# A reordered start in a fused attention and feed-forward kernel: scaling of q, its scores, a padded copy of v and one addition change places

## The chip, the cores and the metric

The kernel runs on one core of one Trainium2 chip, alone. The metric is the device time of one execution in microseconds (us). Four runs of the kernel before gave a median of 559.15 us (557.59 to 560.10).

Five engines work side by side on a core, each with its own queue of instructions: TensorE (PE, with its weight loads shown as PEld), VectorE (DVE), ScalarE (ACT), GpSimd (POOL) and SyncE (SP), which here only issues transfers. Transfers (DMAs) are issued from SP's queue and from ACT's queue.

## The reference

A gated linear attention over 4 batches, 8 heads, 768 tokens and a head size of 48, followed by a two-layer network with an ELU between the layers:

```python
f = 1.0 / (1.0 + np.exp(-f_logit))
for t in range(S):
    state = f[:, :, t, :, None] * state + np.einsum('bhd,bhe->bhde', k[:, :, t], v[:, :, t])
    y[:, :, t] = np.einsum('bhd,bhde->bhe', q[:, :, t], state)
x = y.transpose(0, 2, 1, 3).reshape(B * S, H * D)
h = x @ w_in                                   # 384 -> 2048
g = np.where(h > 0.0, h, np.exp(np.minimum(h, 0.0)) - 1.0)
out = g @ w_out                                # 2048 -> 384
```

The two weight matrices arrive in 64-bit floats; the rest in 32-bit floats.

## The kernel before, in words

The 3072 tokens are cut into 12 units of 256, three to a batch. A unit goes through attention and then through the network; the attention of the next unit is woven between the steps of the network of the one before. Only the start is a stretch without a network to weave into: there the attention of unit 0 has to be finished first. The order of the instructions at the start is written out by hand in `fast` (lines 1079 to 1154); the change lies in it. Later steps are placed by `at_step`.

How attention is computed. Instead of the recurrence, running products of the gates are used. With a = 1 + exp(-f_logit), the running product of a over the tokens of a unit is 1 over the running product of the gates. k is multiplied by it, q by its inverse; then scores are plain products of k and q under a causal mask, and states are plain sums of k times v. The heads lie in four pairs (0 to 3). The tile `f` holds, for each pair, the running product (index 0) and its inverse (index 1). Pair 3 has no rows of its own in the loaded f_logit: its gates arrive packed in the gap rows of pairs 0 to 2 and are spread into place by small transfers.

The helpers that the change and the prediction speak of:

- `gates(u, pieces, bias)` (L612): ACT computes exp(-f) in place (L617) and, unless `bias` is 0, adds one in a second ACT instruction (L619).
- `grow(u, p)` (L628): DVE's running product of pair p (L631). `fall(u, p)` (L633): DVE's inverse of it (L636, 128x256, about 1.7 us each).
- `move(u, which, queue)` (L638): two small transfers (L643) that spread pair 3's running product (`which` 0) or inverse (`which` 1), issued on the queue named.
- `scale(u, ("k" or "q", p, engine))` (L622): k or q of pair p times `f`, in place (L626), here always on POOL.
- `transposed(u, h, bank, pairs)` (L667): PE transposes k (L674), ACT copies the result to `kn` (L678).
- `advance(u, pairs)` (L727): PE's products of `kn` and v, the growth of the states (L737). `step(u, c)` (L686): the states of the four chunks of 64 tokens, one after the other (ACT L697 for the first, DVE L695).
- `scores(u, banks, pairs, pc)` (L703): PE's products of k and q (L714). `mask(u, pc)` (L720): DVE multiplies them by the causal mask (L722); the last part of the scores has to be there.
- `warm(n)` (L1068): n dummy products on PE (L1074) whose result nobody reads; each is two instructions in the profile.
- `first_outputs(part)` (L788): the outputs of unit 0, from masked scores and v in part 0, from states in part 1 (L817). Pair 3's share uses `padded_v` and `padded_s`, copies of v and of the states between columns of zeros, made by POOL (L1113 and L1136); `even_v` (L1098) is another copy of v. ACT and DVE then copy the outputs into `xt` (L827, L829).
- `load(u, names)` (L435): SP's loads of a unit's f, k, q and v. `fetch(n)` (L539): SP's transfer of a piece of the weights into `area`, a staging tile of 7 places (L549, L551, L554). `split`, `lower` and `merge` (L561 to L587) turn such a piece from 64-bit into 32-bit floats, on DVE, ACT and DVE.

What sets the order around the change. Every engine takes its instructions in the order of the program. `fetch(0)` and `fetch(1)` are issued early. The next five stand behind a memset on POOL that clears a few words of `area` (L1142), which in turn stands on POOL behind the last `scale` of unit 0's q and the three copies to `padded_s`. Each transfer signals one of eight semaphores, which are handed out in turn; a transfer that gets a semaphore still in use waits until the transfer before it on that semaphore has landed. The feed-forward network begins with the first up projection (L949), which needs `xt` of unit 0 and the first merged piece of `w_in`. From the second unit on the up projection is split into seven products (L904) on differences of `xt` that POOL makes (`blend`, L892).

Of the kernel before, what the change touches and what calls it, by code (L numbers as in the profile page):

```python
# [356 lines left out]
def fast(ctx: ExitStack, tc: tile.TileContext, q, k, v, f_logit, w_in, w_out, out, flag, outer):  # L357
# [18 lines left out]
    nc = tc.nc  # L376
# [12 lines left out]
    NKT = DM // 128  # L389
# [36 lines left out]
    qkf = [  # L426
        {n: cst.tile([128, HP, 2, U] if n == "f" else [128, HP, U], FP32, name=f"{n}{i}") for n in "fqk"}
        for i in range(NB)
    ]
# [182 lines left out]
    def gates(u, pieces=(NKT,), bias=1):  # L612

        p = 0
        for n in pieces:
            a = qkf[u % NB]["f"][:, p : p + n, 0]
            nc.scalar.activation(a, a, AF.Exp, scale=-1.0)  # L617
            if bias:
                nc.scalar.activation(a, a, AF.Copy, bias=1.0)  # L619
            p += n  # L620

    def scale(u, *todo):  # L622

        t = qkf[u % NB]
        for n, p, e in todo:
            e.tensor_tensor(out=t[n][:, p], in0=t[n][:, p], in1=t["f"][:, p, "kq".index(n)], op=ALU.mult)  # L626

    def grow(u, p):  # L628

        g = qkf[u % NB]["f"][:, p, 0]  # L630
        nc.vector.tensor_tensor_scan(out=g, data0=g, data1=g, initial=1.0, op0=ALU.mult, op1=ALU.max)  # L631

    def fall(u, p):  # L633

        f = qkf[u % NB]["f"]
        nc.vector.reciprocal(f[:, p, 1], f[:, p, 0])  # L636

    def move(u, which, queue):  # L638

        f = qkf[u % NB]["f"]  # L640
        for r in range(2):
            to = PAD + D * r
            queue.dma_start(out=f[to : to + D, NKT, which], in_=f[GAP[r] : GAP[r] + PAD, 0:NKT, which])  # L643
# [23 lines left out]
    def transposed(u, h, bank, pairs=(0, 1)):  # L667

        pairs = [p for p in pairs if u < 2 or 2 * h + p < NKT]
        if 0 in pairs:  # L670
            pts[u, h] = ps.tile([128, 2, NW, 128], FP32, tag=bank, name=f"psT{u}_{h}")
        for p in pairs:
            for w in range(NW):
                nc.tensor.transpose(  # L674
                    pts[u, h][:, p, w], in_=qkf[u % NB]["k"][:, 2 * h + p, w * W : (w + 1) * W], identity=ident[:]
                )
        p, to = slice(pairs[0], pairs[-1] + 1), slice(2 * h + pairs[0], 2 * h + pairs[-1] + 1)
        nc.scalar.copy(kn[:, to], pts[u, h][:, p])  # L678
        if u < 2:
            return  # L680
        gaps = kn[:, NKT, :, MAIN].rearrange("t w (r i j) -> t j w r i", r=2, j=NKT)
        nc.scalar.copy(gaps[:, to], pts[u, h][:, p].rearrange("t p w (a i) -> t p w a i", i=PAD)[:, :, :, 0::7])
# [20 lines left out]
    def scores(u, banks=("a0", "a1"), pairs=range(HP), pc=None):  # L703

        t = qkf[u % NB]
        if pc is None:
            ats[u] = sb.tile([128, 2, NW, HP, C], FP32, tag="at", name=f"at{u}", bufs=1)
            pc = [ps.tile([128, NW, HP, C], FP32, tag=banks[r], name=f"psS{u}_{r}") for r in range(2)]
        for p in pairs:
            for w in range(NW):  # L710
                for b in range(2):
                    cols = slice(w * W + b * C, w * W + b * C + C)
                    for r in range(2):
                        nc.tensor.matmul(  # L714
                            pc[r][FULL[b], w, p], lhsT=t["k"][FULL[r], p, cols], rhs=t["q"][FULL[r], p, cols],
                            start=True, stop=True,
                        )
        return pc
# [8 lines left out]
    def advance(u, pairs=range(HP)):  # L727

        if u not in pus:
            pus[u] = [ps.tile([128, NW, HP, D], FP32, tag=n, name=f"psU{u}_{n}") for n in ("a0", "a1")]  # L730
        pu = pus[u]
        for p in pairs:
            for w in range(NW):
                for r in range(2):
                    h = 2 * p + r
                    for b in range(2):
                        nc.tensor.matmul(  # L737
                            pu[b][FULL[r], w, p], lhsT=kn[FULL[b], p, w, FULL[r]],
                            rhs=vs[u % NB][FULL[b], w, PAD + h * D : PAD + (h + 1) * D],
                            start=(w == 0 and p == 0), stop=(w == NW - 1 and p == HP - 1), skip_group_check=True,  # L740
                        )
# [326 lines left out]
    def warm(n, bank="m0", small=0):  # L1068

        pw = ps.tile([128, 4, 128], FP32, tag=bank, name="psW")  # L1070
        for _ in range(small):
            nc.tensor.matmul(pw[0:1, 0, 0:1], lhsT=ident[:, 0:1], rhs=ident[:, 0:1], start=True, stop=True)
        for _ in range(n):
            nc.tensor.matmul(  # L1074
                pw[:], lhsT=ident[:], rhs=ident[:].unsqueeze(1).broadcast_to([128, 4, 128]), start=True, stop=True
            )
# [15 lines left out]
    fall(0, 0)  # L1092
    scale(0, ("q", 0, nc.gpsimd))
    warm(WA, "m3")
    gates(1, bias=0)
    advance(0, (0, 1))
    pc = scores(0, ("m2", "m3"), (0,))
    nc.gpsimd.tensor_copy(  # L1098
        even_v[:, :, :, PAD:],
        vs[0][:, :, PAD : PAD + NKT * 2 * D].rearrange("t w (p r d) -> t w p r d", r=2, d=D)[:, :, :, 0],  # L1100
    )
    fall(0, 1)
    scale(0, ("k", NKT, nc.gpsimd), ("q", 1, nc.gpsimd))
    fall(0, 2)
    move(0, 1, nc.scalar)
    warm(4)
    transposed(0, 1, "m1", (1,))
    advance(0, (2,))
    scores(0, None, (1,), pc)
    scale(0, ("q", 2, nc.gpsimd))  # L1110
    advance(0, (3,))
    scores(0, None, (2,), pc)
    nc.gpsimd.tensor_copy(  # L1113
        padded_v[:, :, :, PAD : 2 * PAD].rearrange("t w (r j) k -> t w r j k", r=2),
        vs[0][:, :, PAD + NKT * 2 * D : PAD + DM].rearrange("t w (r k j) -> t w r j k", r=2, j=NKT),
    )
    a = qkf[1]["f"][:, 0:NKT, 0]
    nc.vector.tensor_scalar_add(a, a, 1.0)
    for p in range(NKT):
        grow(1, p)  # L1120
    move(1, 0, nc.sync)
    scale(0, ("q", NKT, nc.gpsimd))
    warm(2)
    scores(0, None, (NKT,), pc)
    warm(1)
    fall(1, 0)
    split(0)
    for c in range(NC - 1):
# [88 lines left out]
def kernel(tc, q, k, v, f_logit, w_in, w_out, out):  # L1217

    nc = tc.nc
    with tc.tile_pool(name="flags", bufs=1) as pool:
        flag = pool.tile([1, 1], I32, name="flag")
        store = fast(tc, q, k, v, f_logit, w_in, w_out, out, flag, pool)
        seen = nc.values_load(flag[0:1, 0:1])
        with tc.If(seen < 128) as branch:
            general(tc, q, k, v, f_logit, w_in, w_out, out)
        with branch.Else():
            store(nc.sync, nc.scalar)  # L1230
# [32 lines left out]
```

## Time and profile before

| what | value |
|---|---|
| median of 4 runs | 559.15 us |
| the profiled execution | 558.88 us |
| its span, first to last instruction | 557.1 us |
| PE busy | 541.5 us, 97% |
| DVE busy | 406.9 us, 73% |
| POOL busy | 290.4 us, 52% |
| ACT busy | 228.0 us, 41% |
| granted TensorE clock | 0.999 |
| HBM read, written | 45.02 MB, 4.72 MB |
| chain that ended last | PE 85%, DMA 8%, DVE 3% of the span |
| first up projection (L949) begins | 28.86 us |
| first split product that waits (L904) | 74.83 us |

How to read it. The span is that of one profiled execution, the time is that of the same execution as the host of the runs counts it; they differ by 1.8 us. A row of a timeline gives start, duration, engine, line, operation, output and input tiles and how many; in brackets stands the idle time before it and what ended that. A row of the waits gives who waited for whom: us in total, times, longest. A row of the chain gives start, duration and what held the end at that time. A row of the windows gives the stretch, its length, busy time and count of instructions of PE, PEld, DVE, ACT and POOL, the granted clock, the mean busy share of the 16 DMA engines (which can read slightly over 1) and GB/s. Where an instruction waits for several things, the profile names the one that came last by its own records, and that can be another than the program waits for.

### The profile page before, as it was taken

To read this page: it belongs to the slowest core of one execution; us is meant where nothing else is said; L and a number is where in the kernel's file an instruction comes from. 1 tells how busy PE (TensorE), PEld (TensorE's weight loads), DVE (VectorE), ACT (ScalarE), POOL (GpSimd) and SP (SyncE) were. 2 spreads that over 40 slices of the span, in tenths; PEclk is the share of its full clock that TensorE was granted. 3 is DMA by queue.
4 is the path that set the end of the run, shared out by engine and by line. 5 is a ranking of instruction groups with operands and counts; after the bars stand their busy time and mean duration, and the time that the engine had idled before them with its cause. 6 is when DMAs were issued, how large, how long until landed. Compare 5 with 4: busy or idle time off the path is not lost.

```text
span 557.1 us, 15617 instructions
## 1 busy us (share of the span) xinstructions
PE 541.5 (97%) x6358; PEld 506.6 (91%) x6358; DVE 406.9 (73%) x804; ACT 228.0 (41%) x443; POOL 290.4 (52%) x559
## 2 busy tenths in 40 slices
PE   6799999999999999999999999999999999999996
PEld 3477769999999999999999999999999999999995
DVE  8888997997676776776785785785786687745553
ACT  3288765333434344343434434343343334333331
POOL 6600787484573474375365466357267257325332
PEclk9999999999999999999999999999999999999999
DMA  8998971042034134226216207207308302301001
GB/s 212 253 254 220 290 184 45 4 93 79 3 89 136 35 83 141 63 46 169 73 27 181 81 11 195 81 8 192 88 8 191 88 9 72 88 5 33 31 2 35
DMA packets 39474, 54.30 MB, mean 97 GB/s; under 512 B 4032, under 2 KB 29216, under 8 KB 39392
## 3 DMA queue, kind: packets, MB, share of 16 engines
q1 hardware_dynamic: 38592, 52.61, 36.4%
q8 instruction: 52, 0.85, 0.6%
q10 hardware_dynamic: 800, 0.59, 0.4%
q14 instruction: 30, 0.25, 0.2%
HBM read 45.02 MB, written 4.72 MB: 89 GB/s over the span
## 4 chain that ended last, share of the span: by engine, by line
PE 85%; DMA 8%; DVE 3%; POOL 1%; issue 1%; SPq 1%; ACT 1%; DVEq 0%; ACTq 0%; POOLq 0%
PE psH L904 39%; PE psM L1015 37%; DMA area<-in_moe_w_in_dram 3%; DMA f<-f 2%; PE psY L752 2%; PE psY L772 2%; PE psU_a L737 2%; PE psS L714 2%; PE psT L674 1%; DMA xt<-xt 1%; PE psM L981 1%; DMA f<-in_f_logit_dram 1%; DMA area<-in_moe_w_out_dram 1%; DVE f L636 1%; DVE bits L568 0%
## 5 line engine op out<-in xcount | busy, mean ns | idle before, releaser
L904 PE MATMUL psH<-xt,wi 128*128 128x128 f32 (+1 forms) x1056 | 195.0, 294 | 0.0
L968 POOL TENSOR_TENSOR sums<-gg 128x128 f32<-128x128 f32 x172 | 75.7, 461 | 206.2 <-DVE gg L958 188.7
L936 ACT ACTIVATE gg<-hh 128x512 f32<-128x512 f32 x88 | 55.5, 631 | 248.9 <-DVE hh L926 108.7
L904 PEld LDWEIGHTS psH<-xt,wi 128*128 128x128 f32 x1056 | 149.5, 192 | 1.6
L904 PE MATMUL psH<-xt,area 128*128 128x128 f32 x704 | 121.6, 275 | 1.2 <-POOL xt L892 1.2
L904 PEld LDWEIGHTS psH<-xt,area 128*128 128x128 f32 x704 | 106.5, 191 | 6.0 <-POOL xt L892 1.4
L913 DVE TENSOR_TENSOR hh<-psH,u 128x256 f32<-128x256 f32 x88 | 36.9, 419 | 97.6 <-ACT u L911 97.5
L1015 PE MATMUL psM<-area,sums 128*128 128x192 f32 x516 | 99.9, 326 | 0.1
L1015 PEld LDWEIGHTS psM<-area,sums 128*128 128x128 f32 x516 | 86.0, 190 | 0.3 <-issue 0.2
L1015 PE MATMUL psM<-wo,gg 128*128 128x192 f32 x376 | 77.7, 332 | 0.0
L958 DVE SCALAR_TENSOR_TENSOR gg<-gg,hh 128x512 f32<-128x512 f32 x88 | 63.5, 722 | 1.5 <-ACT gg L937 1.5
L636 DVE RECIPROCAL f<-f 128x256 f32<-128x256 f32 x36 | 62.8, 1748 | 1.3
L937 ACT ACTIVATE gg<-gg 128x512 f32<-128x512 f32 x96 | 60.5, 631 | 3.0
L1015 PEld LDWEIGHTS psM<-wo,gg 128*128 128x128 f32 x376 | 60.2, 190 | 1.3
L926 DVE TENSOR_TENSOR hh<-psH,u43h 128x256 f32<-128x256 f32 (+1 forms) x176 | 54.7, 353 | 3.0
L626 POOL TENSOR_TENSOR q<-q,f 128x256 f32<-128x256 f32 x48 | 40.0, 835 | 20.5 <-DMA area<-in_moe_w_in_dram 14.8
L968 POOL TENSOR_TENSOR sums<-gg,sums 128x128 f32<-128x128 f32 x86 | 45.1, 525 | 6.7
L626 POOL TENSOR_TENSOR k<-k,f 128x256 f32<-128x256 f32 x48 | 40.5, 846 | 8.9 <-DMA f<-f 6.2
L926 DVE TENSOR_TENSOR u43h<-psH,hh 128x256 f32<-128x256 f32 x88 | 37.0, 421 | 9.2 <-PE psH L904 8.8
L968 POOL TENSOR_TENSOR sums<-sums,gg 128x128 f32<-128x128 f32 x86 | 42.6, 495 | 0.0
L1015 PE MATMUL psM<-area,gg 128*128 128x192 f32 x172 | 42.0, 326 | 0.0
L1015 PE MATMUL psM<-wo,sums 128*128 128x192 f32 x172 | 42.0, 326 | 0.0
(102 smaller groups left out, 645.1 us busy)
## 6 DMA issues: line engine op xcount, KB each, us to landing
area<-in_moe_w_out_dram SPq DMA_DIRECT2D x8, 768.0 KB, 10.5
again<-in_moe_w_in_dram SPq DMA_DIRECT2D x16, 384.0 KB, 3.7
again<-in_moe_w_out_dram SPq DMA_DIRECT2D x16, 384.0 KB, 3.6
k<-in_k_dram SPq DMA_DIRECT2D x12, 384.0 KB, 4.4
q<-in_q_dram SPq DMA_DIRECT2D x12, 384.0 KB, 5.6
v<-in_v_dram SPq DMA_DIRECT2D x12, 384.0 KB, 5.8
area<-in_moe_w_in_dram SPq DMA_DIRECT2D x8, 576.0 KB, 8.6
out_dram<-o SPq DMA_DIRECT2D x42, 96.0 KB, 1.9
```

The source lines that it names most:

```text
L626: e.tensor_tensor(out=t[n][:, p], in0=t[n][:, p], in1=t["f"][:, p, "kq".index(n)], op=ALU.mult)
L636: nc.vector.reciprocal(f[:, p, 1], f[:, p, 0])
L714: nc.tensor.matmul(pc[r][FULL[b], w, p], lhsT=t["k"][FULL[r], p, cols], rhs=t["q"][FULL[r], p, cols], start=True, stop=True,)
L737: nc.tensor.matmul(pu[b][FULL[r], w, p], lhsT=kn[FULL[b], p, w, FULL[r]], rhs=vs[u % NB][FULL[b], w, PAD + h * D : PAD + (h + 1) * D], sta ...
L904: nc.tensor.matmul(to, lhsT=lhs, rhs=rhs, start=(n == 0), stop=True, skip_group_check=True)
L913: add = lambda to, x, y: nc.vector.tensor_tensor(out=to, in0=x, in1=y, op=ALU.add)
L926: add = lambda to, x, y: nc.vector.tensor_tensor(out=to, in0=x, in1=y, op=ALU.add)
L936: nc.scalar.activation(g[:], h, AF.Relu, scale=-1.0)
L937: nc.scalar.activation(g[:], g[:], AF.Exp, scale=-1.0)
L958: nc.vector.scalar_tensor_tensor(out=g[:], in0=g[:], scalar=-1.0, in1=phs.pop(P), op0=ALU.add, op1=ALU.max)
L968: nc.gpsimd.tensor_tensor(out=s[:, i], in0=x, in1=y, op=op)
L1015: nc.tensor.matmul(pm[bank][:, half * DH : (half + 1) * DH], lhsT=x, rhs=y, start=first, stop=(j == NP - 1), skip_group_check=True,)
```

## The change

Three things are changed in the hand-written start, all within `fast`:

1. `gates(1)` lets ACT add the one. DVE's addition (L1118) is removed.
2. The inverses of pairs 1 and 2 of unit 0 are each followed at once by the scaling of that pair's q on POOL, one dummy product and that pair's scores on PE. The scaling of k of pair 3, which waits for the first move, stands behind them on POOL. The state products of pair 2 stand ahead of them on PE. The four dummy products behind the scores of pair 0 are spread: one ahead of the scores of each of the pairs 1 and 2, three behind them, and two ahead of the last scores, none behind the last scores. There are seven of them in both versions.
3. The copy to `padded_v` stands on POOL behind the scaling of q of pair 3 and no longer ahead of it.

```diff
-    gates(1, bias=0)
+    gates(1)
     advance(0, (0, 1))
     pc = scores(0, ("m2", "m3"), (0,))
     nc.gpsimd.tensor_copy(even_v ...)
-    fall(0, 1)
-    scale(0, ("k", NKT, nc.gpsimd), ("q", 1, nc.gpsimd))
-    fall(0, 2)
+    advance(0, (2,))
+    for p in range(1, NKT):
+        fall(0, p)
+        scale(0, ("q", p, nc.gpsimd))
+        warm(1)
+        scores(0, None, (p,), pc)
     move(0, 1, nc.scalar)
-    warm(4)
+    scale(0, ("k", NKT, nc.gpsimd))
+    warm(3)
     transposed(0, 1, "m1", (1,))
-    advance(0, (2,))
-    scores(0, None, (1,), pc)
-    scale(0, ("q", 2, nc.gpsimd))
     advance(0, (3,))
-    scores(0, None, (2,), pc)
-    nc.gpsimd.tensor_copy(padded_v ...)
-    a = qkf[1]["f"][:, 0:NKT, 0]
-    nc.vector.tensor_scalar_add(a, a, 1.0)
+    warm(2)
     for p in range(NKT):
         grow(1, p)
     move(1, 0, nc.sync)
     scale(0, ("q", NKT, nc.gpsimd))
-    warm(2)
     scores(0, None, (NKT,), pc)
-    warm(1)
+    nc.gpsimd.tensor_copy(padded_v ...)
     fall(1, 0)
```

Besides this, the semaphores of some early transfers come out otherwise in the built program: SP's load of unit 1's k waits for the last piece of unit 1's f instead of v; the second half of unit 0's second move waits for v; the second half of unit 1's first move waits for that k instead of the second half of unit 0's second move; and the third weight fetch waits, besides the memset, for the second half of unit 0's second move instead of k.

## The prediction
> **What bounds the kernel now.** I read the windows of the whole run first, then the chain of waits up to 75 us, then the timeline of each engine and SP's queue of transfers over the first 29 us, and last the built program's list of instructions with the semaphores each waits for. The windows show one long stretch that TensorE fills, and a start that it does not:
>
> ```profile
> 21.00:29.00 8.00, 4.87 (x171) 3.35 (x171) 7.30 (x10) 2.06 (x5) 4.91 (x6) 1.00 1.01 247
> 29.00:45.00 16.00, 15.57 (x97) 12.29 (x98) 14.43 (x22) 13.83 (x14) 0.73 (x1) 1.00 1.03 238
> 45.00:75.00 30.00, 28.67 (x347) 20.48 (x346) 25.77 (x39) 24.40 (x27) 15.09 (x21) 1.00 0.85 232
> 75.00:557.00 482.00, 476.72 (x5590) 462.99 (x5590) 342.42 (x713) 180.00 (x389) 255.69 (x492) 1.00 0.29 76
> ```
>
> The first column after the stretch is PE's busy time. From 75 us on it is 476.7 of 482 us and the change touches nothing there, so only the moment at which that stretch begins can move. Between 29 and 75 us PE is idle for 0.43 + 1.33 = 1.76 us. The chain of waits says what holds its beginning:
>
> ```profile
> 13.88 5.55 DMA f<-f
> ...
> 19.58 0.21 POOL q L626
> ...
> 20.25 0.62 POOL padded_s L1136 x3
> 20.86 0.06 POOL area L1142
> 20.92 0.02 issue
> 20.94 0.32 SPq L551
> ...
> 23.76 10.08 DMA area<-in_moe_w_in_dram
> ...
> 38.63 7.30 DMA f<-f
> ...
> 74.83 0.38 PE psH L904
> ```
>
> Unit 0's second small move (L643) lands at 19.46; GpSimd scales the last q (L626, pair 3), copies the padded states (L1136) and clears a few words of the staging area (L1142); only then may SP send the third weight fetch (L551). From there on it is the stream of weight transfers, with the engines' DMA share near 1 and each next issue waiting for a landing, up to PE's last early wait. SP's waits and PE's timeline confirm both ends:
>
> ```profile
> SPq L442 <- DMA v<-in_v_dram: 0.9, 1, 0.9
> SPq L551 <- POOL area L1142: 0.8, 1, 0.8
> 74.83 0.49 PE L904 MATMUL psH<-xt,area 128*128 128x128 f32 x2 [1.24 <-POOL xt L892]
> 28.86 2.86 PE L949 MATMUL psH<-xt,wi 128*128 128x256 f32 x12 [1.66 <-DVE xt L829]
> ```
>
> So two paths meet at 74.83: the weight stream, which ends last, and PE's own work since 28.86, which has 1.24 us of slack there. A delay of the stream is paid in full; a delay of the first up projection only beyond 1.24 us.
>
> **The change part by part, times of the profiled execution.**
>
> *The added one* (0.62 us on DVE at 13.16, L1118) becomes an ACT instruction of 128x768. The same form takes 0.84 us later in the run (L619). ACT's exponential runs 11.22 to 12.07, so the sum is there by 12.95; behind it ACT has the move that waits for DVE's third inverse, done at 13.24. Cost 0, covered by 0.3 us; without the cover each us would go onto the chain. DVE's three scans start 0.62 us earlier, but pair 2's q on GpSimd now runs beside them (a scan took 0.69 us alone and 1.15 beside GpSimd at 7.22). What they release, SP's move of unit 1 (L643), waited at 18.10 for a landing and still does. Gain 0 to 0.6, on nothing that ends last: 0.
>
> *q pair by pair.* Inverses end at about 9.95, 11.60 and 13.24 (three in 4.94 us from 8.30). GpSimd scales q of pair 1 at 11.7 and of pair 2 at 13.3 (0.73 us each, 1.13 beside a scan) instead of after 16.16. That work moves out of the interval 16.16 to 17.58, where GpSimd was going to wait for the move until 19.46 anyway. Gain 0.
>
> *PE's order.* One dummy product is two instructions 0.427 us apart (12.34, 12.77, 13.19). Seven go in both versions. Now: scores 0 until 11.8, states of pair 2 to 12.1, one dummy to 12.96, scores 1 (0.31) to 13.3, a dummy to 14.1, scores 2 at 14.2 to 14.5, then three dummies, 2.56 us, to 17.1 to 17.4. The transposes of pair 3 stood at 16.25 and now start there; as before, 0.96 us later (16.25 to 17.21) its key copy is in place: 18.1 to 18.4; with 0.31 for the state products and 1.71 for two dummies PE is free at 20.1 to 20.4. The last scores wait for q at 20.30 and stood at 20.36: 0 to 0.1 us late. The dummy behind them ended at 21.87, while the next products were released by the mask (DVE) at 21.7 to 21.8: taking it away gains at most 0.1. Together 0 on PE, whose slack covers 1.24.
>
> *A transfer changes place without a line of the diff.* In the list of waits, SP's load of unit 1's k (L442, at 10.96) no longer waits for v (the 0.9 us above) but for unit 1's last piece of f, landed by 9.78. It goes at about 10.0, ahead of the second half of unit 0's first move, which ACT issues from 10.32. Landings follow the order of issue across both queues here: the halves of that move, issued from 9.56, landed at 14.65 and 14.93, after the fetch parts issued before them (13.39 to 14.41), and k at 16.17. With k in front the second half lands 1.24 us later, near 16.2. Queued behind: key pair 3 on GpSimd (15.06 becomes 16.3, done by 17.05 to 17.45, hidden under the dummies above; uncovered it would cost 1.24), and on SP the second fetch's parts, 14.67 and 15.03, which wait for those two landings. The engines have q, v and the second move to do until 19.44, so its data need not flow before then; a load issued at 13.45 first moved bytes about 2 us on. Cost 0 as long as it goes out before 17.4. SP's second half of unit 1's move, at 19.46, waits for k instead of unit 0's move and goes about 0.7 us earlier, before anything that ends last: 0.
>
> On this the Trainium skill speaks otherwise ("DMA: Bandwidth & Descriptors", section "Queues, rings and completion order"): each DMA engine alternates between the queues packet by packet. By that rule a small move on ACT's queue would slip in between SP's packets and k in front of it would cost next to nothing; by the landings it costs 1.24 us. The sum is the same by both, since either is hidden; I go by the landings.
>
> *v's padded copy behind.* This one is on the chain. GpSimd's L1113 took 0.77 us at 17.52, beside DVE's L568 and L572; the copy of even heads (L1098), larger, took 0.42 with no such neighbour. It now stands between q's last scale (ends 20.30) and the padded states, and DVE is idle from about 19.7 until the mask at 20.94, so the value is nearer 0.42. The three small copies (0.62) then run partly beside the mask; by the ratio of GpSimd's k row (1.13 against 0.73) they grow by up to 0.34. So the clearing of the area, and the third fetch with all behind it on SP, is later by 0.42 to 1.11 us; I take 0.6. Lower bound 0: if the engines still had bytes to move. They had not:
>
> ```profile
> 20.00:21.00 1.00, 0.64 (x18) 0.58 (x18) 0.06 (x1) 0.68 (x1) 1.00 (x6) 1.00 1.08 249
> 21.00:22.00 1.00, 1.00 (x6) 0.24 (x5) 1.00 (x2) 0.00 (x0) 1.00 (x2) 1.00 1.01 169
> 22.00:23.00 1.00, 0.85 (x48) 0.72 (x44) 0.97 (x3) 0.00 (x0) 1.00 (x3) 1.00 0.87 151
> 23.00:24.00 1.00, 0.51 (x25) 0.28 (x18) 1.00 (x2) 0.00 (x0) 0.76 (x1) 1.00 1.01 325
> ```
>
> The last column is GB/s: it sinks from 249 to 151 before the third fetch flows, so its delay lengthens the hole one for one. Later stations keep their order (the move at 38.63 is issued by ACT behind PE's work and lands after what SP had sent), so the stream is 0.6 later at 74.83.
>
> Sum: 0 + 0 + 0 + 0 + 0.6. The span goes from 557.1 to 557.7. The profiled execution itself took 558.88, 1.8 around the span and 0.27 under the median of 559.15; I add 0.6 to the median: 559.75, by the bounds 559.15 to 560.3.
>
> **The rivals.**
> *Starved twice (slower).* Place: SP's queue between 14.67 and 17.4. If both halves of unit 0's first move land behind k and SP's three issues (0.31, 0.56, 0.59 with their waits) end past 17.4, the second fetch flows late as well. Price: up to the 1.6 us that separate 14.67 from 16.25, plus 0.6 to 0.7: +2.3, 561.4. For it: SP is strictly in order and k is 384 KB. Against: 1.1 us of cover. It decides from 17.4 on.
> *Clock.* With the dummy behind the last scores gone, PE has a hole of about 0.9 us at 20.8 on top of 0.86 at 23.5 and 1.66 before 28.86. If the granted clock fell, the 3.6 us of products from 21.8 to 27.2 would double (cold dummies stood 0.85 apart): +3.6, less 1.24 of slack, 561.5. Against: the clock stayed at 1.00 over every stretch above, those holes included.
> *Hidden (no change).* Bytes left of the second fetch, itself later now, fill the hole at 21 to 23: 559.15.
> *The move overtakes v (faster).* Move and v were issued together at 13.88, and v landed 0.3 us ahead (19.12). If the move wins, q's last scale is 1.2 us earlier, less 0.6 for the padded copy: 558.55; if states are early too, at most PE's idle 1.76 is gained: 557.4.
>
> **How the numbers follow.** Forecast 0.43, starved twice 0.25, clock 0.06, hidden 0.12, overtaking 0.14. A measurement of this kernel can tell 0.3%, 1.68 us, from no change. The forecast and the hidden case lie inside, and half of overtaking nearly so; the runs of before scatter over 2.5 us, which takes a little from each. Slower 0.32, same 0.55, faster 0.13. The range: down to 557.7 for most of overtaking, up to 562.0 for starved twice with scatter. The forecast's own range is 558.7 to 560.8.
>
> **What would show it.** The third fetch issued at 21.4 to 21.9 rather than 20.94, with GB/s low between 21 and 24; unit 1's k issued near 10.0 and key pair 3 scaled near 16.3; the last scores still near 20.4; PE's wait at the first split product (L904) 0.4 to 1.1 us longer and ending that much later. Wrong if the third fetch keeps 20.94, if the last q is scaled well before or after 19.6, or if PE's clock dips.

## The result and the profile after

| | before | changed kernel |
|---|---|---|
| median | 558.96 us (557.07 to 560.39, 76 runs) | 559.88 us (558.06 to 562.82, 50 runs) |
| ratio, 95% interval | | 1.0019 [1.0012, 1.0025] |
| profiled execution, its span | 558.88, 557.1 us | 559.26, 557.5 us |

By the medians the change costs 0.92 us. (The ratio here and below is the estimate recorded with its interval; it is not the quotient of the two medians, which is 1.0016 here.) The forecast was 559.75. Its number held by luck: the padded copy from which it was added up shows no cost in the profile. The windows of the changed kernel (columns as before: stretch, length, PE, PEld, DVE, ACT, POOL, granted clock, DMA share, GB/s):

```profile
21.00:29.00 8.00, 4.55 (x186) 3.43 (x184) 6.95 (x9) 2.84 (x6) 4.50 (x7) 1.00 1.06 252
29.00:45.00 16.00, 15.25 (x96) 12.26 (x97) 13.71 (x21) 13.47 (x14) 0.73 (x1) 1.00 1.06 241
45.00:75.00 30.00, 29.13 (x347) 20.49 (x345) 26.86 (x40) 24.29 (x25) 14.54 (x20) 1.00 0.86 232
75.00:557.00 482.00, 477.06 (x5590) 463.32 (x5590) 342.20 (x713) 180.78 (x389) 255.98 (x493) 1.00 0.29 76
```

The long stretch is as full as before. The loss lies ahead of it. The chain of waits has another course there:

```profile
9.70 5.61 DMA f<-f
...
15.32 9.19 DMA area<-in_moe_w_in_dram
24.53 0.39 SPq L549
...
24.96 9.78 DMA area<-in_moe_w_in_dram
...
75.26 0.82 PE psH L904 x5
```

GpSimd's last scaling of q, its copies and the third fetch, through which the chain ran before, are gone from it. It now goes over unit 0's first move, the second weight fetch that is issued when it lands (15.32), and the transfer of `w_out` (L549) that waits for that fetch. Four lines of SP's timeline before, then SP's timeline and one of its waits in the changed kernel:

```profile
10.96 0.32 SPq L442 DMA_DIRECT2D k<-in_k_dram  x1
13.45 0.32 SPq L442 DMA_DIRECT2D q<-in_q_dram  x1
...
15.03 1.20 SPq L554 DMA_DIRECT2D area<-in_moe_w_in_dram  x2
...
23.13 0.59 SPq L549 DMA_DIRECT2D area<-in_moe_w_out_dram  x1
```

```profile
10.27 0.53 SPq L442 DMA_DIRECT2D k<-in_k_dram  x1
14.10 0.32 SPq L442 DMA_DIRECT2D q<-in_q_dram  x1
...
15.32 0.42 SPq L551 DMA_DIRECT2D area<-in_moe_w_in_dram  x1
17.07 1.20 SPq L554 DMA_DIRECT2D area<-in_moe_w_in_dram  x2
...
21.07 0.32 SPq L551 DMA_DIRECT2D area<-in_moe_w_in_dram  x1
...
24.53 0.39 SPq L549 DMA_DIRECT2D area<-in_moe_w_out_dram  x1
```

```profile
SPq L549 <- DMA area<-in_moe_w_in_dram: 1.8, 1, 1.8
```

Unit 1's k left at 10.27, ahead of the second half of the first move (ACT, 10.46). That half landed at 17.06, right behind k (16.84), instead of at 14.93. The next part of the second fetch waits for it and the last part stands behind: issued from 17.07 instead of 15.03, and the fetch landed by 25.23 instead of 23.98; its first part, the one that L549 waits for, landed at 24.51 instead of 21.82. That first part does not wait for k or for the late half: it left at 15.32 instead of 14.67 and took 9.19 us to land instead of 7.15. What goes with that slowness is shown below, at e5 and e6. The third fetch itself left at 21.07, 0.13 later than before, and yet L549, next in the queue, waited 1.8 us for the second: 24.53 instead of 23.13. POOL:

```profile
17.19 0.94 POOL L626 TENSOR_TENSOR k<-k,f 128x256 f32<-128x256 f32 x1 [2.82 <-DMA f<-f]
18.36 0.76 POOL L626 TENSOR_TENSOR q<-q,f 128x256 f32<-128x256 f32 x1 [0.24 <-DMA f<-f]
19.08 0.44 POOL L1119 COPY padded_v<-v 128x192 f32<-128x192 f32 x1
20.03 0.96 POOL L1133 COPY padded_s<-state 128x48 f32<-128x48 f32 x3 [0.51 <-ACT state L697]
20.93 0.10 POOL L1139 MEMSET area<- 128x5 int32 x1
```

The padded copy (0.44 us) is followed by 0.51 us of waiting for the states. Without the copy POOL would have waited that much longer: in this execution it costs nothing. And the last q is scaled 1.2 us earlier than before (18.36 against 19.58), because both halves of unit 0's second move (ACT, 13.18 and 13.80) now stand ahead of SP's q (14.10; before, q left at 13.45, between them). They landed at 17.96 and 18.30, q at 20.25. How far this comes from the edit is open: q leaves just after the first part of the first weight fetch has landed, here at 14.03 instead of 13.39, and over all 14 profiles that landing lies anywhere from 13.39 to 14.55, with k early (13.42 to 14.03) or not. The gift is not passed on either. Two lines of PE's and two of DVE's timeline before, then those of the changed kernel:

```profile
16.25 0.44 PE L674 MATMUL psT<-ident,k 128*128 128x128 f32 x2 [0.75 <-POOL k L626]
...
20.36 0.46 PE L714 MATMUL psS<-q,k 64*64 64x64 f32 x16 [0.36 <-POOL q L626]
```

```profile
20.94 1.29 DVE L722 TENSOR_TENSOR at<-psS,twice 128x512 f32<-128x512 f32 x2 [1.58 <-POOL area L1142]
...
28.25 0.55 DVE L829 COPY xt<-psY 64x384 f32<-64x384 f32 x1 [0.60 <-ACT xt L829]
```

```profile
15.37 2.84 PE L1074 MATMUL psW<-ident 128*128 128x512 f32 x6
18.18 0.44 PE L674 MATMUL psT<-ident,k 128*128 128x128 f32 x2
19.08 0.45 PE L737 MATMUL psU_a<-v,kn 64*64 64x48 f32 x16 [0.46 <-ACT kn L678]
19.46 1.98 PE L1074 MATMUL psW<-ident 128*128 128x512 f32 x4
21.38 0.46 PE L714 MATMUL psS<-q,k 64*64 64x64 f32 x16
...
29.16 2.86 PE L949 MATMUL psH<-xt,wi 128*128 128x256 f32 x12 [2.02 <-DVE xt L829]
...
75.26 0.49 PE L904 MATMUL psH<-xt,area 128*128 128x128 f32 x2 [0.87 <-POOL xt L892]
```

```profile
21.96 1.29 DVE L722 TENSOR_TENSOR at<-psS,twice 128x512 f32<-128x512 f32 x2 [1.27 <-PE psS L714]
...
28.55 0.55 DVE L829 COPY xt<-psY 64x384 f32<-64x384 f32 x1
```

The last scores have their q at 19.12, but stand behind pair 3's transposes (18.18 instead of 16.25) and two dummies: 21.38 instead of 20.36. The transposes follow the three dummies ahead of them without a gap, just as the late k is ready (18.13); in e7 and e12, with k scaled by 15.9 and 16.4, they stand at 17.91 and 18.18 all the same. The mask follows (21.96 instead of 20.94), and all of DVE's work behind it. Before, the copy to `xt` waited 0.60 us for ACT; now it follows DVE's own work without a gap, 0.30 later, and the first up projection with it. PE's hole ahead of that grew from 1.66 to 2.02 us.

### The profile page after: what moved, and what is told of

Its sections match the earlier page's. It is cut to its first block, busy times and chain, and to the rows that moved or that the text cites. A ratio compares the mean times of both kernels' runs of the same rounds, so it can differ in the third digit from the quotient of the medians.

```text
span 557.5 us, 15617 instructions
## 1 busy us (share of the span) xinstructions
PE 542.1 (97%) x6358; PEld 506.8 (91%) x6358; DVE 406.7 (73%) x803; ACT 229.1 (41%) x444; POOL 289.6 (52%) x559
## 4 chain that ended last, share of the span: by engine, by line
PE 86%; DMA 9%; DVE 1%; POOL 1%; ACT 1%; issue 0%; SPq 0%; DVEq 0%; ACTq 0%; POOLq 0%
PE psH L904 39%; PE psM L1015 37%; DMA area<-in_moe_w_in_dram 5%; PE psY L752 2%; PE psY L772 2%; PE psU_a L737 2%; DMA area<-in_moe_w_out_dram 2%; PE psS L714 2%; PE psT L674 1%; DMA f<-f 1%; DMA xt<-xt 1%; PE psM L981 1%; PE psW L1074 1%; DVE wi L586 0%; POOL xt L892 0%
## 5 line engine op out<-in xcount | busy, mean ns | idle before, releaser
L626 POOL TENSOR_TENSOR q<-q,f 128x256 f32<-128x256 f32 x48 | 39.8, 829 | 20.4 <-DMA f<-f 16.0
```

## The experiments

What the theories of the expectations are. The copy (C, the forecast's own): v's padded copy holds the third fetch. The transfer (T): with `gates(1)` the eight semaphores are handed out otherwise, and unit 1's k goes ahead of the first move. Others put the cost on the new order (PE's products, its instruction transfer), on the third fetch as such, or on the granted clock. Every experiment had 12 executions against 35 of the kernel before on the same chip (its medians 559.04 for e1 to e4, 559.14 for e5 to e8, 559.23 for e9 to e12). The last column counts executions with a mean granted clock of 0.996 or less: in the profiles these are the ones in which the clock halved for one or two stretches of 3.41 us during the start (0.991 to 0.996; all others 0.997 or more). The line is not sharp: in the profiles the clock is also halved for up to the last 3.1 us of the span, which alone takes up to 0.003 off the mean. For the changed kernel the clock of 52 executions is on record, but not on which chip they ran. A profile shows one of the twelve executions, and that one can lie far from their median: 0.94, 1.39 and 1.18 us above it in e2, e3 and e4, 1.16, 1.36, 1.28 and 1.24 us below it in e1, e7, e8 and e9. So the traces show what waits for what; the price has to come from the medians and ratios.

| kernel | median us | ratio, 95% interval | clock 0.996 or less |
|---|---|---|---|
| before, all of them | | | 16 of 105 |
| changed | 559.88 | 1.0019 [1.0012, 1.0025] | 21 of 52 |
| e1, padded copy alone | 559.20 | 1.0002 [0.9989, 1.0015] | 2 of 12 |
| e2, gates alone | 559.82 | 1.0014 [1.0000, 1.0028] | 4 of 12 |
| e3, order alone | 560.11 | 1.0019 [1.0005, 1.0032] | 4 of 12 |
| e4, all but gates | 560.34 | 1.0017 [0.9998, 1.0035] | 3 of 12 |
| e5, before, more PE instructions | 559.55 | 1.0010 [0.9997, 1.0023] | 11 of 12 |
| e6, e3 less five dummies | 559.50 | 1.0013 [1.0002, 1.0023] | 10 of 12 |
| e7, changed, first move ahead of k | 560.55 | 1.0023 [1.0010, 1.0036] | 8 of 12 |
| e8, e2, first move ahead of k | 559.15 | 1.0004 [0.9989, 1.0020] | 0 of 12 |
| e9, before, memset earlier | 559.48 | 1.0006 [0.9988, 1.0025] | 1 of 12 |
| e10, before, memset later | 559.30 | 1.0002 [0.9987, 1.0018] | 2 of 12 |
| e11, changed, memset earlier | 560.24 | 1.0018 [1.0002, 1.0033] | 6 of 12 |
| e12, changed, three dummies more | 559.71 | 0.9998 [0.9980, 1.0017] | 0 of 12 |

**e1: only the padded copy moves.**

```diff
     scores(0, None, (2,), pc)
-    nc.gpsimd.tensor_copy(padded_v ...)
...
     scores(0, None, (NKT,), pc)
     warm(1)
+    nc.gpsimd.tensor_copy(padded_v ...)
```

> The kernel before with only v's padded copy moved behind the scaling of q of pair 3. Theory C (the copy delays the third weight fetch): the memset at 20.80 and the third fetch's issue at 20.94 move 0.4 to 1.1 us later, the time rises by about 0.6 us (ratio 1.0007 to 1.0018). Rival T (the load of unit 1's k ahead of unit 0's first move does the harm): that load stays at 10.96 here, ratio 1.000. Rival D (dummy products hold up pair 3 and the last scores): ratio 1.000.

POOL's timeline of e1:

```profile
19.08 0.73 POOL L626 TENSOR_TENSOR q<-q,f 128x256 f32<-128x256 f32 x1 [1.35 <-DMA f<-f]
19.75 0.44 POOL L1122 COPY padded_v<-v 128x192 f32<-128x192 f32 x1
20.13 0.62 POOL L1136 COPY padded_s<-state 128x48 f32<-128x48 f32 x3
20.70 0.11 POOL L1142 MEMSET area<- 128x5 int32 x1
```

The copy does lie on POOL between the last q and the memset, 0.38 us of it. But in this execution the move landed 0.5 us earlier, and the third fetch left at 20.83. The median shows no cost, but the interval reaches 1.0015, or 0.84 us: the 0.6 us of the forecast are not excluded.

**e2 and e8: the addition on ScalarE alone, then with the old order of transfers.** e2:

```diff
-    gates(1, bias=0)
+    gates(1)
...
-    nc.vector.tensor_scalar_add(a, a, 1.0)
```

e8 is e2, and unit 0's first move is issued by SP ahead of unit 1's k:

```diff
-    load(1, "kqv")
-    for n in range(1, HOLD):
-        fetch(n)
     warm(W0, "m3")
...
-    move(0, 0, nc.scalar)
+    move(0, 0, nc.sync)
+    load(1, "kqv")
+    for n in range(1, HOLD):
+        fetch(n)
```

> The kernel before with only the added one on ScalarE. In the built program this edit alone lets the load of unit 1's k go without waiting for v. Theory C: ratio 1.000. Rival T: the load goes near 10.2, unit 0's first move lands near 15.3 and 17 instead of 14.65 and 14.93, key pair 3 is scaled near 17.2 instead of 15.06, and the time rises by 0.5 to 1 us (ratio 1.001 to 1.002). Rival D: ratio 1.000.

> The kernel before with the added one on ScalarE, and unit 0's first move issued by SP ahead of the load of unit 1's k. Theory T: what e2 lost (1.0014) comes back, ratio 0.999 to 1.0005, with key pair 3 scaled near 15 us and the instruction fetch near 21. Rival (the added one on ScalarE itself costs): ratio 1.001 or more, as e2.

The scaling of pair 3's k, on POOL, in e2 and then in e8:

```profile
17.35 0.84 POOL L626 TENSOR_TENSOR k<-k,f 128x256 f32<-128x256 f32 x1 [5.14 <-DMA f<-f]
```

```profile
16.07 1.06 POOL L626 TENSOR_TENSOR k<-k,f 128x256 f32<-128x256 f32 x1 [3.60 <-DMA f<-f]
```

In e2 k left at 10.17 and the first move landed at 17.21; the first up projection began at 30.09. With the move ahead of k it landed at 15.93, the up projection began at 28.61, and the median is that of the kernel before. So ACT's addition shows no cost of its own, and what it does to the order of the transfers costs about 0.1% there. The two intervals overlap: the traces show the mechanism, the medians agree with it and do not prove it. Nor does the price carry over to the changed kernel: in e2 the late k stands on POOL ahead of the scaling of q of the pairs 1 and 2 and holds them up, in the new order it stands behind them. And the second fetch is not late in e2: its held parts left at 17.23 and 17.84, as in the changed kernel, but its first part landed at 22.86, 7.72 us after its issue.

**e3 and e4: the new order alone, and all but the gates.** e3 is the changed kernel with DVE's addition back and the padded copy ahead of the last q; e4 has DVE's addition back only.

> The kernel before with only the new order of pairs, scores and dummy products; the added one on VectorE, the padded copy ahead of the last scaling of q. Theory C: ratio 1.000, transposes of pair 3 about 1 us later than 16.25 and hidden. Rival T: ratio 1.000. Rival D: the transposes start near 17.2 to 18.2 and the last scores are held by the two dummies ahead of them, 0.5 to 1 us on the time (ratio 1.001 to 1.002).

> The changed kernel with the added one back on VectorE, so that the load of unit 1's k waits for v again. Theory C: as slow as the changed kernel, ratio to the kernel before 1.001 to 1.002. Rival T: ratio 1.000. Rival D: ratio 1.001 to 1.002, with the last scores later than 20.36.

Neither has k ahead of the move, and both have a higher median than the kernel before (for e4 the interval, from 0.9998, just includes no change). POOL's scaling of the last q in e3, and the windows of e3:

```profile
22.36 0.72 POOL L626 TENSOR_TENSOR q<-q,f 128x256 f32<-128x256 f32 x1 [4.62 <-DMA f<-f]
```

```profile
21.00:25.00 4.00, 0.96 (x21) 0.52 (x20) 1.28 (x3) 0.43 (x1) 2.64 (x7) 1.00 0.47 76
25.00:29.00 4.00, 3.48 (x126) 3.17 (x128) 3.93 (x7) 0.33 (x2) 3.13 (x5) 0.60 0.97 237
```

Unit 0's second move landed at 22.22 instead of 19.44, the DMA engines ran dry (76 GB/s), and PE, idle meanwhile, had its clock halved from 25.84 to 29.25. The up projection began at 31.82 (32.98 in e4), and at the split product PE had 0.18 us of wait left, in e4 none: PE's own path has become the bound in these two executions. By the ratios the parts do not add: gates (1.0014) and order (1.0019) together give no more than order alone; but the intervals are too wide to exclude that they do. The profiled execution of the changed kernel, where the second move passed q and v, was spared this. e11 and e12, with k sent about as early (9.96 and 10.46), were not: their last q was scaled at 20.29 and 20.71.

**e5 and e6: is it PE's instruction transfer?** The trace has a queue for instructions (16 KB a packet); before, its first packet in this stretch was at 21.28 us, in e3, e4 and the changed kernel at 15.2 to 15.4. e5 moves it there by more instructions on PE in the kernel before (45 products of one element for three dummies), e6 takes the dummies ahead of the transposes out of e3.

```diff
-    warm(4)
+    warm(1, small=45)
```

```diff
     for p in range(1, NKT):
         ...
-        warm(1)
         scores(0, None, (p,), pc)
     ...
-    warm(3)
     transposed(0, 1, "m1", (1,))
```

> The kernel before, its order of scores and transfers untouched; of the four dummy products behind the scores of pair 0 three are replaced by 45 one-column dummies that take about the same time (29 ns for each of 90 instructions), so that TensorE gets further in its stream of instructions by 15 us. Theory F (the 16 KB piece of TensorE's instructions, fetched at 21.3 in the kernel before and at 15.2 in the reordered ones, holds one DMA engine for 1.3 us and with it unit 0's second move): the fetch shows near 15 us or earlier, the second half of that move lands at 20.5 to 22.5 instead of 19.44, the last q of unit 0 is scaled after 20.6 and the ratio is 1.001 to 1.003. Rival D (the order of dummies and transposes itself): fetch or not, ratio 1.000.

> The new order alone, as in e3, without the five dummy products that stand ahead of the transposes of pair 3 (the two ahead of the last scores stay). TensorE is then less far in its stream when it waits for key pair 3. Theory F: the instruction fetch comes after 16.5 us, unit 0's second move lands near 19.5 again and the ratio is 1.000 to 1.001, unless the clock falls for want of work. Rival D: the transposes start near 15.8 to 16.7 instead of 18, ratio 1.000. If the fetch stays near 15 us, F expects 1.001 to 1.002 and D 1.000.

In e5 the packet moved to 15.34, so it is PE's, but the last q was scaled at 19.83, much as before (19.58), and the time is at most 0.23% longer. In e6 the packet stayed at 15.18 and the second move passed q and v as in the changed kernel (last q at 18.22). The early packet alone does not make the second move late. Of the seven kernels in the new order five have the last q at 20.04 to 22.71 (e3, e4, e7, e11, e12); the seven in the old order have it at 18.53 to 19.91. By the time of the packet, though, the 14 profiles part cleanly. Where it is early (14.95 to 15.65: the seven kernels in the new order, and e5), the first part of the second fetch takes 8.87 to 9.80 us from issue to landing; where it is late (20.29 to 22.82: the other six), 7.15 to 7.78. The second move sorts by it too. Sent 0.30 us or more ahead of q (the changed kernel, e6, e8, e9), its second half landed at 17.75 to 18.30 either way; otherwise it landed at 18.94 to 19.65 with the late packet and at 19.70 to 22.58 with the early one. Since e5 changes nothing but PE's instructions, this points to the early packet as what slows the transfers under way then. What that costs in time e5 does not show: its interval starts at 0.9997, and 11 of its 12 executions had the low clock.

**e7: the changed kernel with the first move ahead of k** (the edit of e8).

> The changed kernel, with unit 0's first move issued by SP ahead of the load of unit 1's k (and of the loads behind it), so that k no longer goes in front of it; semaphores of the early transfers come out in the plain order. Theory T (k in front of the first move is part of the cost): key pair 3 is scaled near 15 us instead of 17.2 and the ratio falls from 1.0019 to 1.001 or less. Theory F: the instruction fetch stays near 15.3, and with the second move behind q and v again it lands after 20.5; ratio 1.0015 to 1.003.

It did not get the time back. SP's and PE's timelines of e7:

```profile
17.48 3.04 SPq L554 DMA_DIRECT2D area<-in_moe_w_in_dram  x2
```

```profile
28.89 4.29 PE L949 MATMUL psH<-xt,wi 128*128 128x256 f32 x12 [2.08 <-DVE xt L829]
```

The move landed early, but the semaphores shifted again: now the parts of the second fetch wait for the second move, which landed at 17.46 and 19.91, and the last q was late (20.04). PE's hole of 2.08 us was followed by a half clock from 30.16 to 33.58, so that the first up projection took 4.29 instead of 2.86 us. Undoing one hold brought another.

**e9, e10, e11: is it the third fetch at all?** e9 and e11 put the memset behind the last q scale in the kernel before and in the changed one; e10 puts two more copies to `padded_v` ahead of it in the kernel before.

```diff
     scale(0, ("q", NKT, nc.gpsimd))
+    nc.gpsimd.memset(area[:, HOLD:].bitcast(I32)[:, :, 0:1], 0)
...
-    nc.gpsimd.memset(area[:, HOLD:].bitcast(I32)[:, :, 0:1], 0)
```

```diff
+    nc.gpsimd.tensor_copy(padded_v ...)
+    nc.gpsimd.tensor_copy(padded_v ...)
     nc.gpsimd.memset(area[:, HOLD:].bitcast(I32)[:, :, 0:1], 0)
```

> The kernel before with one edit: the memset that lets the third weight fetch go stands right behind the last q scale, ahead of the three padded_s copies. Third-fetch theory (the forecast's link: the later this fetch, the later the stream of weights and the end, one for one): fetch issued near 19.3 instead of 20.94, so the split product and the end up to 1.6 us earlier, 557.5 to 558.4. Rival (the fetch before still feeds the DMA engines, so that a third fetch between 19 and 21 is not what they wait for): 558.8 to 559.4, no change, and DMA busy between 21 and 25 us the same.

> The kernel before with two more copies of the last pair's v into padded_v on POOL ahead of that memset (0.44 us each, so about 0.9 us, the same values again): a delay of the size the forecast feared, doubled, and put where nothing can hide it. Third-fetch theory: issued near 21.8, end 0.6 to 0.9 us later, 559.7 to 560.0. Rival (not what the engines wait for): no change, 558.8 to 559.4.

> The changed kernel with the memset right behind the last q scale, ahead of the padded copies. Third-fetch theory: fetch near 19.3 instead of 21.07, time falls from 559.9 to 558.3 to 559.2. Rival (the cost lies in the order of the earlier transfers: k in front of unit 0's first move, second fetch landed 24.5 to 25.2 instead of 21.8 to 24.0): stays 559.6 to 560.2.

In e9 the fetch left at 19.65, 1.29 earlier, in e10 at 22.04, 1.10 later (0.9 of it by the copies). Not all of that is the edit. In e9 the last q was scaled 1.04 earlier by itself; from its end to the fetch 0.64 us became 0.07, so the edit's share is 0.57, and in e10 it is 0.9. One for one these shares would be ratios of 0.9990 and 1.0016. Each lies just inside its interval, so neither median alone excludes them. Against each other the two kernels would have to lie 1.47 us apart; the mean of e10 is 0.21 us below that of e9, with 0.9 us to either side for 95%, and that does exclude it. The chain and the waits of e9 say where the gain went in its profile:

```profile
15.52 7.78 DMA area<-in_moe_w_in_dram
...
23.31 0.39 SPq L549
...
23.75 9.81 DMA area<-in_moe_w_in_dram
```

```profile
SPq L549 <- DMA area<-in_moe_w_in_dram: 2.0, 1, 2.0
```

L549 was sent at 23.31 instead of 23.13: with the third fetch out of the way, the landing of the second one holds it. In this execution that landing was late, at 23.30 instead of 21.82, partly since the second fetch itself left 0.85 later. In the kernel before 1.3 us lay between it and L549. And in e10:

```profile
22.04 0.32 SPq L551 DMA_DIRECT2D area<-in_moe_w_in_dram  x1
...
23.70 0.58 SPq L549 DMA_DIRECT2D area<-in_moe_w_out_dram  x1
```

Of 1.10 us, 0.57 is left at L549, since before SP's last part of the third fetch took 1.12 us to issue, here 0.59. So the third fetch was on the chain of the kernel before, with the second fetch behind it by up to 1.3 us. e11 says less than it was meant to: unit 0's second move was late in it, and the third fetch left at 21.25, no earlier than in the changed kernel.

**e12: the clock.** Three dummies fill PE's hole ahead of the first up projection.

```diff
     first_outputs(1)
+    warm(3)
     lower(1)
```

> The changed kernel with three more dummy products (about 1.4 us) on PE between the last product of the first unit's outputs (near 27.1) and the first up projection (29.16), where PE stands idle for 2.0 us. Clock theory: of the changed kernel's 52 executions 21 show a mean granted clock of 0.996 or less, of the 70 of the kernel before run beside the experiments 8, and those are 0.6 to 1.2 us longer; if the hole makes these windows, their share falls to one in ten and the median by 0.2 to 0.4 us, to 559.5 to 559.7. Rival (windows come from elsewhere, or cost nothing): same share, 559.7 to 560.1; 560.2 or more if the dummies delay the up projection.

```profile
27.19 2.84 PE L1074 MATMUL psW<-ident 128*128 128x512 f32 x6
29.87 2.75 PE L949 MATMUL psH<-xt,wi 128*128 128x256 f32 x12
```

This is PE's timeline of e12: the dummies took 2.84 us, twice what the expectation reckoned, and leave no hole. None of the 12 executions has the low clock, against 21 of 52, so with the hole filled the halved clock did not occur. What that gains is less clear: the ratio is 0.9998, but by the medians alone it would be 1.0009. It beats the changed kernel perhaps (the intervals overlap between 1.0012 and 1.0017), the kernel before not.

## Why the prediction was right, and where it was not

The sum was 0 + 0 + 0 + 0 + 0.6, and the time 0.92 longer (0.73 above the median it was added to). The number is close because the term put at 0.6 showed no cost and something that the sum put at nothing did. Point by point:

- *That only the start can move* held. Over the 14 profiled kernels the span goes from 556.1 to 559.8 us, while from the first split product on `area` to the end it is always 482.0 to 483.0 (482.25 before, 482.28 in the changed kernel). The difference of the two profiles arises before that product.
- *The padded copy, 0.6, and the third fetch behind it*: this step failed. The third fetch left at 21.07, not 21.4 to 21.9, since the copy fitted into a wait for the states. The medians of e1 show no cost, though its interval has room for 0.6, and e9 and e10 taken together show that a shift of this fetch is not paid one for one. The hole at 21 to 24 us that was to grow was filled by the late second fetch: 233, 190 and 236 GB/s against 169, 151 and 325.
- *The transfer that changes place, 0*: what the term says of the transfers came (k at 10.0, was 10.27; second half of the move later), the size not: 2.13 us later instead of 1.24. The condition named was that the second fetch goes out before 17.4; of its held parts one left at 17.07, the other at 17.68, and it landed with L549 waiting. That is the place of the rival "starved twice", at a price of 1.40 us on SP at L549, of which 0.43 arrived at the split product of the profiled execution. But k's new place is not what made that landing late: e2 has the same change of place and no late landing, e6 and e12 have the late landing (24.69 and 24.72) without k ahead of the move, and e7, with the move ahead of k again, did not get the time back. The step that failed is that the landing of the second fetch was reckoned from its issue alone: it also took 2.04 us longer on the way, as in all profiles with the early instruction packet of PE. By the Trainium skill's round robin by packets ("DMA: Bandwidth & Descriptors", "Queues, rings and completion order") one would expect k in front to cost little. Here a 48 KB transfer with 384 KB in front of it on the other queue landed 2.13 us later, 0.22 behind those 384 KB; its own packets on ACT's queue began at 14.99 instead of 13.22. The measurement decides.
- *Overtaking*, another rival, happened as well: the second move passed q and v, and q's last scale came 1.2 us earlier, as forecast. It gained nothing, because the scores were held on PE. That landings follow the order of issue, on which the prediction went, holds only in part: before, q left at 13.45 and landed at 17.71, ahead of the first half of the second move (13.27, landed at 18.03).
- *PE's order, 0 to 0.1*: failed. The three dummies took 2.84 us from 15.37, not 2.56 from 14.5; pair 3's transposes came at 18.18 instead of 17.1 to 17.4, and the last scores at 21.38 instead of 20.4. The slack at the split product took it (0.87 us of wait left of 1.24). That the new order also moves PE's instruction packet from 21.28 to 15.36 us stands in no term.
- *The added one, 0*: right in itself as far as the runs show (done at 13.12, the move issued at 13.18; e8).
- *The clock*: the profiled execution shows 1.00 throughout, so the rival seemed refuted; over all executions it was not. Its share is 21 of 52 against 16 of 105. Those executions are 0.62 us longer than the others (559.79 on average) in the changed kernel and 1.21 (558.98) before, so the larger share explains 0.25 x 0.62 to 1.21 = 0.16 to 0.30 us. Among the executions without it, 0.81 us of difference remain. The 16 of 105 are from the chips of the experiments, so a difference between chips is not excluded from these figures.

What stays open: how those 0.81 us divide between the late second fetch, which all seven profiles of the new order show, and the late second move, which five of them show (e3, e4, e7, e11, e12). The single profiled pair has 0.38 of them, and the intervals of 12 executions, some 0.3% wide, can't separate parts of 0.1%. That the early packet causes both rests on how the profiles sort and on e5's alone; no run measures its price apart from the clock.

## What to carry to other kernels

An edit that moves work between engines can change which semaphore a transfer waits for, and so the order of transfers that no line of it names: compare the waits of the built programs, and price the transfer that falls behind, not only the one that goes ahead. An engine's instructions arrive by transfers too: another order of PE's work moved one of them from 21 to 15 us, into the transfers that were under way there. A wait that the chain shows has a next one behind it; what removing or lengthening it by a microsecond is worth can't be said until the landing that holds the next issue of the queue is known. One profile is one draw: here a landing that no edit aimed at moved by 1.2 us between profiles and decided which of two transfers went first. And a profile at full clock says only that this execution was spared: look at the clock of all of them.

## What the runs showed of the hardware

A rule of the clock can be read off these traces. In the profiles the granted clock changes on a grid of 3.41 us. Between 12 and 45 us, every grid window at full clock in which PE was busy for 0.89 to 1.57 us was followed by one at half clock (e3 1.57, e4 0.89, e5 1.44, e6 0.95, e7 1.33), and none in which it was busy for 1.70 us or more. So for products of some size the bound lies between 46% and 50% of the window. At half clock it lies elsewhere: in e4 a window with 2.43 us busy was followed by another at half clock, windows with 2.95 us and more by full clock. One window earlier, e5 shows an exception: from 11.51 to 14.92 the profile has PE busy all the time, most of it with the 45 products of one element, and a half clock followed. In this one case such products were no cover. The Trainium skill ("TensorE: Matmul & The Clock Gate", Part 1) gives a free-running window of 3413 ns, which agrees, and a fall after an idle window; here 1.84 us of idleness in a window (e3) was enough. The grid does not start with the program: its first full-clock window begins 6.3 to 8.8 us into the span, another time in each profile. So a hole costs only in those executions where a window lies over it. Sliding a window of that length over the start of the profiled executions: before, no position has less than 1.70 us busy; in the changed kernel, with 2.02 us idle ahead of the up projection instead of 1.66, 14 of 24 positions have 1.39 to 1.62; with e12's dummies none has less than 2.01. The kernel before stood just above the bound, and 0.36 us more of idle time took it below. Single profiles only hint at the share (e10: 14 of 24 positions, but 2 of 12 executions; e11: none, but 6 of 12).
